# Squares of batch 2's first eight chunks taken by channel behind the first blocks, and the first group of x issued ahead of the third expert's weights

## The chip, the cores and the metric

The kernel runs on one core of a Trainium2 chip. The metric is the device time of one execution in microseconds (us), a median of several runs. The engines are TensorE (PE, with PEld for its weight loads), VectorE (DVE), ScalarE (ACT), GpSimd (POOL) and SyncE (SP), which here issues all ordinary DMAs in one queue, in program order. POOL issues the indirect DMAs (scatters).

## The reference, cut to what matters

```python
# q, k, v: (4, 5056, 256) f32; tau scalar; w_gate (256, 8); w1 (8, 256, 1024); w2 (8, 1024, 256)
qn = q / (np.linalg.norm(q, axis=1, keepdims=True) + 1e-06)   # by channel, over the 5056 tokens
kn = k / (np.linalg.norm(k, axis=1, keepdims=True) + 1e-06)
a = softmax(kn.transpose(0, 2, 1) @ qn / tau)                 # (4, 256, 256)
x = (v @ a).reshape(20224, 256)
expert_idx = np.argmax(x @ w_gate, axis=1)
for e in range(8):
    xe = x[expert_idx == e]
    out[expert_idx == e] = gate_w * (np.maximum(xe @ w1[e], 0.0) @ w2[e])
```

## The kernel before, in words

**Attention.** For each batch, `attention` loads q and k in 20 chunks of 256 tokens (`raw`, 512 KB each, L205). PE adds each chunk's products into two accumulators `sp` (L225 for a chunk taken as it is in f32, L229 and L230 for a chunk that is first split into a high and a low part `hl` by ACT, L188, and DVE, L189). For the norms ACT squares every chunk (L215 or L217) and DVE adds the squares into `ssq` (L218); after the last chunk PE sums `ssq` over the partitions (`ntp`, L245), so the norm is one number for each channel. A softmax follows, and then ten groups of 512 tokens of x: PE makes four tiles `px` (L365 for the first batch), ACT copies them and takes their squares (L370, L372), ACT and DVE write the two halves of the rows (L386, L387), some small DVE operations route the tokens (L395 to L442), and POOL scatters the rows to `xs` in HBM (L445).

**Weights.** `weights` loads eight experts in 32 loads of 512 KB (L120), 4 for an expert. PE takes a gram matrix of each (L158), DVE and PE make a scale from it (L162, L123, L84), and ACT and DVE split the weights in place in sixteen steps (L112 and L113).

**Blocks.** Tokens sorted by expert are run in blocks of 256: SP reads a table entry (L581), then loads the rows transposed (`xT`, L586) and their factors (`mt`, L588). A block has 48 `hp` products (L616), 48 `y` products (L638), ACT's and DVE's `ht` (L623, L624), ACT's `o` (L651) and two scatters to `out` by POOL (L653). `xT` and `mt` have three buffers each: the fourth block's `xT` waits for the first block's `hp`, its `mt` for the first block's scatters.

**Order.** The program is written as generators. In the opening each step takes one step of the first batch's attention (a group of x takes two steps, its half groups), then a number of weight loads, then, from step 23 on, a chunk of batch 2. The first block needs the first six groups of x, all weights and a table (`ctp`, L505). The remaining chunks of batch 2 are spread over the first three blocks. A scheduler then orders each engine's instructions. The `raw` and `vraw` tiles of batch 2 and of the first batch's last groups of x share one ring of three buffers (`RAW = 3`), taken strictly in turn; a load into a buffer waits on SP until its last reader is done, and all later loads of SP wait behind it. In the text chunks of batch 2 are numbered from 0; chunks 0 and 14 to 19 are split, chunks 1 to 13 are not.

The lines that set the opening's order and the chunk's work are these:

```python
second = attention(1, [i == 0 or i >= NATIVE for i in range(nch)], True, normal)
...
weighed += take(wts, 0 if step < nch else min(14 if step == nch else 2, 4 * E + 1 - weighed))
...
raw = work.tile([P, 2, 512], F32, tag=tag, name="raw", bufs=bufs)
load = sync.dma_start(out=raw, in_=qk[b, ch])
```

Of the kernel before, what the change touches and what calls it, by code (L numbers as in the profile page):

```python
# [10 lines left out]
F32 = mybir.dt.float32  # L11
F32R = mybir.dt.float32r
F16 = mybir.dt.float16
BF16 = mybir.dt.bfloat16
I32 = mybir.dt.int32
AF = mybir.ActivationFunctionType
ALU = mybir.AluOpType
AX = mybir.AxisListType
ENG = mybir.EngineType

P = 128
B, N, C = 4, 5056, 256
NP = 5120
E, F = 8, 1024
# [3 lines left out]
BLK = 256  # L28
G = 10
T = 4  # L30
CUT = 6

SORTED = [CUT * T * P] + [N * (b + 1) for b in range(B)]
# [27 lines left out]


@with_exitstack
def attention_then_experts(ctx, tc, qk, vT, wts_in, kc, out):
    nc = tc.nc
    sync, act, vec, pool, pe = nc.sync, nc.scalar, nc.vector, nc.gpsimd, nc.tensor

# [112 lines left out]
    RAW = 3  # L180
    WP = 5
    EARLY = 2
    NATIVE = 14
# [5 lines left out]
        vec.tensor_tensor(out=hl[:, 1], in0=raw, in1=hl[:, 0], op=ALU.subtract)  # L189
        return hl  # L190

    def attention(b, s_split, x_split, acc):

# [5 lines left out]
        for ch in range(nch):  # L201

            tag, bufs = (("raw", RAW), ("rows", 3), ("xg", 2), ("raw", RAW), ("rows", 3))[ch % 5 if b == 0 else 0]
            raw = work.tile([P, 2, 512], F32, tag=tag, name="raw", bufs=bufs)
            load = sync.dma_start(out=raw, in_=qk[b, ch])  # L205
            if b == 0:
                last_load[0] = load.ins
            hl = None
            if s_split[ch]:
                hl = split(raw)  # L210
                sq = raw
            else:
                sq = work.tile([P, 2, 512], F32, tag="hl", name="sq", bufs=2)
            if ch == 0:
                act.activation(ssq, raw, AF.Square)  # L215
            else:
                act.activation(sq, raw, AF.Square)  # L217
                vec.tensor_tensor(out=ssq, in0=ssq, in1=sq, op=ALU.add)  # L218
            def products(ch=ch, raw=raw, hl=hl):
                for j in range(2):  # L220
                    first, last = ch == 0 and j == 0, ch == nch - 1 and j == 1
                    for c in range(2):
                        kc0 = C + c * P
                        if not s_split[ch]:
                            pe.matmul(  # L225
                                sp[c][:, 0, :], raw[:, j, kc0 : kc0 + P], raw[:, j, 0:C], start=first, stop=last
                            )
                            continue
                        pe.matmul(sp[c], hl[:, 0, j, kc0 : kc0 + P], hl[:, :, j, 0:C], start=first, stop=False)  # L229
                        pe.matmul(  # L230
                            sp[c][:, 1, :], hl[:, 1, j, kc0 : kc0 + P], hl[:, 0, j, 0:C], start=False, stop=last
                        )


            if b > 0 or ch < nch - 2:
                products()
            else:
                behind.append(products)
            yield 2 * 640
# [10 lines left out]
            return tiny.tile([P, 4], F32, name=name)  # L250

        ss, y, h = four("n_ss"), four("n_y"), four("n_h")
        vec.tensor_scalar(out=ss, in0=tp[:, 0:4], scalar1=1e-30, scalar2=None, op0=ALU.max)

        vec.tensor_scalar(
            out=y.bitcast(I32), in0=ss.bitcast(I32), scalar1=-0.5, scalar2=float(0x5F3759DF), op0=ALU.mult, op1=ALU.add
# [408 lines left out]
    def take(gen, n):  # L665
        for _ in range(n):
            next(gen, None)
        return n
# [2 lines left out]
    normal = [(ps_a, "acc")] * 2  # L671
    wts = weights()
    first = attention(0, [False] * nch, False, [(ps_y, "y0"), (ps_y, "y1")])
    second = attention(1, [i == 0 or i >= NATIVE for i in range(nch)], True, normal)

    ones16 = one.tile([P, P], F16, name="ones16")
    vec.memset(ones16, 1.0)
# [28 lines left out]
    weighed = 0  # L706
    for step in range(2, nch + 1 + 2 * CUT):
        take(first, 1)
        weighed += take(wts, 0 if step < nch else min(14 if step == nch else 2, 4 * E + 1 - weighed))
        if step > nch + 2:  # L710
            take(second, 1)
    tables = {0: table(0)}
# [85 lines left out]
```

## Time and profile before

| | us |
|---|---|
| median of 3 runs | 1186.41 |
| lowest and highest | 1183.15, 1186.71 |
| the profiled execution | 1188.32 |
| its span, first to last instruction | 1186.6 |
| PE busy in the span | 1153.5 (97%) |
| PE busy from 240 to 1180 us | 936.50 of 940 |
| PE busy from 40 to 139.5 us | 82.01 of 99.5 |
| start of the first block on PE | 139.49 |
| start of batch 2's norm sum on PE (`ntp`) | 191.48 |

The table's busy times are read from the profile by stretch. A PE that is busy nearly all the time after 240 us means that work moved there is paid for in full, and that a delay before it is carried to the end.

### The profile page before, as it was taken

The page shows a single profiled execution, that of the slowest core. Times are in us where ns is not written, and L with a number is a line of the kernel's source. Part 1 is how long each engine was busy: PE and PEld are TensorE (multiplying, and loading weights), DVE is VectorE, ACT ScalarE, POOL GpSimd, SP SyncE. Part 2 cuts the span into 40 slices and gives each one's busy share as a digit, 9 for nine tenths or more (in the row PEclk, how much of TensorE's full clock was granted, in tenths as well). Part 3 has the DMA queues.
Part 4 walks back from the last instruction along what each step waited for, and adds up shares of the span by engine and source line. Part 5 has one row for each costly group of instructions (what it writes and reads, how often), then busy time and mean ns, then how long its engine had stood idle before and what let it go on. Part 6 is the DMA issues. An engine that isn't in the chain of part 4 may idle for free.

```text
span 1186.6 us, 28182 instructions
## 1 busy us (share of the span) xinstructions
PE 1153.5 (97%) x10242; PEld 1024.9 (86%) x10242; DVE 899.4 (76%) x2384; ACT 643.5 (54%) x1362; POOL 392.3 (33%) x366
## 2 busy tenths in 40 slices
PE   9798899999999999999999999999999999999998
PEld 8677688899888889999888889999988888889897
DVE  6789988778887877777888777776875566656886
ACT  6399854877655536665565536666533223332232
POOL 0046761466511123544422212455421111112121
PEclk9989989999999999999999999999999999999999
DMA  9977765445555524444354434443242222111121
GB/s 340 408 277 254 208 177 134 135 122 145 139 145 120 130 81 101 118 115 119 97 152 127 131 91 93 131 95 82 70 109 50 50 55 55 46 51 38 40 52 35
DMA packets 147871, 145.93 MB, mean 123 GB/s; under 512 B 115980, under 2 KB 117393, under 8 KB 147728
## 3 DMA queue, kind: packets, MB, share of 16 engines
q1 hardware_dynamic: 132336, 102.48, 33.0%
q0 software_dynamic: 15392, 41.60, 9.8%
q8 instruction: 82, 1.34, 0.5%
q14 instruction: 61, 0.50, 0.1%
HBM read 80.03 MB, written 43.29 MB: 104 GB/s over the span
## 4 chain that ended last, share of the span: by engine, by line
PE 57%; issue 24%; DVE 7%; POOL 5%; ACT 3%; DMA 3%; SPq 1%; POOLq 0%; DVEq 0%; ACTq 0%
PE y L638 20%; PE hp L616 19%; PE px L368 7%; POOL out L653 4%; PE sp L225 4%; PE sp L229 3%; DMA raw<-in_qk 2%; PE sp L230 2%; DVE W L113 1%; ACT xjunk L372 1%; PE px L365 1%; DVE rows L387 1%; DVE hl L189 1%; ACT W L112 1%; ACT xg L370 1%
## 5 line engine op out<-in xcount | busy, mean ns | idle before, releaser
L616 PE MATMUL hp<-xT,wp 128*128 128x256 f16 (+1 forms) x4320 | 450.0, 262 | 1.6 <-DVE ht L624 1.1
L638 PE MATMUL y<-wp,ht 128*128 128x256 f16 x3888 | 447.7, 273 | 0.0
L616 PEld LDWEIGHTS <-wp 128*128 128x128 f16 x4320 | 383.1, 98 | 46.1 <-issue 3.4
L638 PEld LDWEIGHTS <-ht 128*128 128x128 f16 x3888 | 373.9, 98 | 53.3 <-issue 4.7
L653 POOL DMA_INDIRECT out<-o,mt x162 | 184.9, 1141 | 628.5 <-ACT o L651 595.2
L604 DVE COPY wp<-W 128x1024 f16 x720 | 297.8, 425 | 116.0 <-PE y L638 65.3
L623 ACT ACTIVATE ht<-hp 128x512 f16<-128x512 f32 x324 | 191.6, 593 | 157.1 <-PE hp L616 143.1
L624 DVE SCALAR_TENSOR_TENSOR ht<-hp,ht 128x512 f16<-128x512 f32 x324 | 219.6, 686 | 22.6 <-ACT ht L623 16.6
L445 POOL DMA_INDIRECT xs<-rows,r_si x160 | 189.5, 1184 | 122.7 <-issue 41.8
L651 ACT ACTIVATE o<-y,b_fac 128x256 f32<-128x256 f32 x162 | 68.8, 470 | 207.2 <-PE y L638 196.6
L368 PE MATMUL px<-a_h,hl 128*128 128x264 f32 x480 | 98.1, 296 | 0.0
L386 ACT ACTIVATE rows<-xg,x_sc 128x256 f16<-128x256 f32 x160 | 69.9, 497 | 25.7 <-DVE r_ex L419 16.0
L368 PEld LDWEIGHTS px<-a_h,hl 128*128 128x128 f32 x480 | 78.8, 188 | 1.6 <-issue 0.6
L189 DVE TENSOR_TENSOR hl<-raw,hl 128x1024 fp32r<-128x1024 f32 x47 | 57.4, 1221 | 26.7 <-ACT hl L188 26.7
L188 ACT CAST hl<-raw 128x1024 fp32r<-128x1024 f32 x47 | 49.1, 1044 | 45.2 <-PE sp L230 38.2
L229 PE MATMUL sp<-hl 128*128 128x512 f32 x188 | 72.3, 418 | 1.1 <-DVE hl L189 1.1
L225 PE MATMUL sp<-raw 128*128 128x256 f32 x264 | 65.3, 403 | 7.5 <-DMA raw<-in_qk 7.5
L387 DVE SCALAR_TENSOR_TENSOR rows<-xg,x_sc,rows 128x256 f16<-128x256 f32 x160 | 69.5, 477 | 1.2 <-ACT rows L386 0.8
L217 ACT ACTIVATE raw<-raw 128x1024 f32<-128x1024 f32 x44 | 46.6, 1058 | 42.6 <-DVE hl L189 42.4
L372 ACT ACTIVATE xjunk<-xg 128x256 bf16<-128x256 f32 x160 | 66.7, 417 | 3.2
L368 PE MATMUL px<-a_l,hl 128*128 128x264 f32 x240 | 68.2, 284 | 0.0
L225 PEld LDWEIGHTS sp<-raw 128*128 128x128 f32 x264 | 52.0, 202 | 15.9 <-DMA raw<-in_qk 8.6
(144 smaller groups left out, 926.4 us busy)
## 6 DMA issues: line engine op xcount, KB each, us to landing
raw<-in_qk SPq DMA_DIRECT2D x80, 512.0 KB, 4.2
vraw<-in_vT SPq DMA_DIRECT2D x34, 512.0 KB, 5.1
W<-in_w SPq DMA_DIRECT2D x28, 512.0 KB, 8.5
v<-in_vT SPq DMA_DIRECT2D x12, 256.0 KB
out<-o,mt POOLq DMA_INDIRECT x162, 2.4
xs<-rows,r_si POOLq DMA_INDIRECT x160, 4.0
wraw<-in_w SPq DMA_DIRECT2D x4, 512.0 KB, 6.5
xT<-xs SPq DMA_TRANSPOSE x90, 3.9
```

The source lines that it names most:

```text
L225: pe.matmul(sp[c][:, 0, :], raw[:, j, kc0 : kc0 + P], raw[:, j, 0:C], start=first, stop=last)
L229: pe.matmul(sp[c], hl[:, 0, j, kc0 : kc0 + P], hl[:, :, j, 0:C], start=first, stop=False)
L368: pe.matmul(px, hl[:, vh, c, ts], ah[:, c, :], start=(n == 0), stop=(n == 5))
L372: act.activation(junk, xg[:, t, 0:C], AF.Square, accum_out=ss[:, t : t + 1])
L387: vec.scalar_tensor_tensor(out=r16[:, t, C : 2 * C], in0=x, scalar=sc[:, t : t + 1], in1=r16[:, t, 0:C], op0=ALU.mult, op1=ALU.subtract,)
L445: ins = pool.indirect_dma_start(out=xs[:, :], out_offset=bass.IndirectOffsetOnAxis(ap=si[:n, t : t + 1], axis=0), in_=rows[:n, t, :], in_o ...
L604: copied[0] = vec.tensor_copy(out=t, in_=Wf[:, ds(e * 8192 + n * 1024, 1024)]).ins
L616: pe.matmul(hp[:, f % nf, :], wp[:, dc, wh, (f % 2) * P : (f % 2 + 1) * P], xT[:, 2 * xh + dc, :], start=(n == 0), stop=(n == 5),)
L623: act.activation(ht[:, 0], hp, AF.Relu)
L624: vec.scalar_tensor_tensor(out=ht[:, 1], in0=hp, scalar=0.0, in1=ht[:, 0], op0=ALU.max, op1=ALU.subtract)
L638: pe.matmul(ys[j], hts[f // nf][:, hh, f % nf, j * P : (j + 1) * P], wp[:, f % 2, wh, :], start=(f == 0 and n == 0), stop=(f == 7 and n == 2),
L653: pool.indirect_dma_start(out=out[:, :], out_offset=bass.IndirectOffsetOnAxis(ap=mt.bitcast(I32)[:, j, 1:2], axis=0), in_=o, in_offset=Non ...
```

## The change

**Squares by channel.** Batch 2's chunks 0 to 7 no longer get a square on ACT and an add on DVE. Instead q and k of these eight chunks (2048 tokens) are stored a second time, transposed, as `qkT`: channels in partitions, 1024 tokens in a row. `own_squares` loads such a tile `row` (512 KB, in the same ring as `raw`), and ACT squares it in place and sums along the row (`accum_out`) into `parts`. It is called eight times, behind the load of chunks 10 to 17. After the chunks `parts` is reduced by one small DVE operation and added to the norm sum. Chunk 8 starts `ssq`, chunk 9 is the first to add.

**Chunk 0.** It is no longer split. The accumulators are cleared by a product of a zero tile `none` (one DVE memset, two f16 products of 512 columns) in place of the first product's start.

**Order of the opening.** Ten weight loads instead of fourteen stand ahead of the first group of x, then two loads twice, and three loads at each further step instead of two.

```diff
+ASIDE = 8
...
+    parts = tiny.tile([P, 4, 2], F32, name="n_parts", bufs=1)
+
+    def own_squares(n):
+
+        row = work.tile([P, ASIDE * P], F32, tag="raw", name="row", bufs=RAW)
+        sync.dma_start(out=row, in_=qkT[n // 2, n % 2])
+        act.activation(row, row, AF.Square, accum_out=parts[:, n // 2, n % 2 : n % 2 + 1])
+
+    def attention(b, s_split, x_split, acc, aside=0):
...
-            else:
+            elif ch >= aside:
                 sq = work.tile([P, 2, 512], F32, tag="hl", name="sq", bufs=2)
-            if ch == 0:
+            if ch == 0 and aside:
+                none = work.tile([P, 512], F16, tag="o", name="none", bufs=2)
+                vec.memset(none, 0.0)
+                for s_ in sp:
+                    pe.matmul(s_.rearrange("p s c -> p (s c)"), none[:, 0:P], none, start=True, stop=False)
+            if aside and nch - 10 <= ch < nch - 2:
+                own_squares(ch - (nch - 10))
+            if ch == aside:
                 act.activation(ssq, raw, AF.Square)
-            else:
+            elif ch > aside:
                 act.activation(sq, raw, AF.Square)
                 vec.tensor_tensor(out=ssq, in0=ssq, in1=sq, op=ALU.add)
...
-                    first, last = ch == 0 and j == 0, ch == nch - 1 and j == 1
+                    first, last = ch == 0 and j == 0 and not aside, ch == nch - 1 and j == 1
...
+        if aside:
+            vec.tensor_reduce(out=h, in_=parts, axis=AX.X, op=ALU.add)
+            vec.scalar_tensor_tensor(out=ss, in0=tp[:, 0:4], scalar=1e-30, in1=h, op0=ALU.max, op1=ALU.add)
...
-    second = attention(1, [i == 0 or i >= NATIVE for i in range(nch)], True, normal)
+    second = attention(1, [i >= NATIVE for i in range(nch)], True, normal, ASIDE)
...
-        weighed += take(wts, 0 if step < nch else min(14 if step == nch else 2, 4 * E + 1 - weighed))
+        weighed += take(wts, 0 if step < nch else min(10 if step == nch else 2 if step < nch + 3 else 3, 4 * E + 1 - weighed))
```

**Where the instructions stand.** On SP, at the start of the blocks, the last load of x of the first batch (`vraw`) was followed by chunk 10, and then came the first block's loads:

```order
L349 DMA vraw_1567<-in_vT 128x1024
L205 DMA raw_1708<-in_qk 128x1024
L581 TENSOR_LOAD c_tb_1333
L586 ISA
L586 DMA_TRANSPOSE xT_1339<-xs_78 128x4x256
```

Now the first block's loads come directly, and chunk 10 (`raw_1683`) is issued only after the third block's:

```order
L607 DMA_TRANSPOSE xT_1637<-xs_78 128x4x256
L609 ISA
L609 DMA mt_1639<-xs_78 128x2x2
L215 DMA raw_1683<-in_qk 128x1024
L198 DMA row_1686<-in_qkT 128x1024
L215 DMA raw_1731<-in_qk 128x1024
```

So chunk 10 has moved behind the loads of three blocks, while on PE its products stand behind the first 12 `hp` products both before and now.

On SP, between the third block's `mt` and the fourth block's `mt`, there stood before seven loads of chunks (11 to 17):

```order
L588 DMA mt_1664<-xs_78 128x2x2
L205 DMA raw_1753<-in_qk 128x1024
L205 DMA raw_1797<-in_qk 128x1024
L205 DMA raw_1835<-in_qk 128x1024
L205 DMA raw_1896<-in_qk 128x1024
L581 TENSOR_LOAD c_tb_1333
L586 ISA
L586 DMA_TRANSPOSE xT_1892<-xs_78 128x4x256
L205 DMA raw_1947<-in_qk 128x1024
L205 DMA raw_2011<-in_qk 128x1024
L205 DMA raw_2065<-in_qk 128x1024
L588 ISA
```

Now a `row` stands behind each chunk (the first five of the eleven loads of this stretch are shown with the fence above and this one):

```order
L198 DMA row_1734<-in_qkT 128x1024
L215 DMA raw_1778<-in_qk 128x1024
L602 TENSOR_LOAD c_tb_1308
L607 ISA
L607 DMA_TRANSPOSE xT_1879<-xs_78 128x4x256
L198 DMA row_1781<-in_qkT 128x1024
L215 DMA raw_1819<-in_qk 128x1024
L198 DMA row_1822<-in_qkT 128x1024
L215 DMA raw_1883<-in_qk 128x1024
L198 DMA row_1888<-in_qkT 128x1024
L215 DMA raw_1937<-in_qk 128x1024
L609 ISA
```

Chunks 16 and 17, which stood ahead of the fourth block's `mt`, have moved behind it.

On DVE, ahead of the first table (`c_ni`), the sixth group's routing ended so, with a step of the weights' split and an add of squares between the group's one-hot rows and its slots `r_si`:

```order
L416 TENSOR_REDUCE r_ex<-r_ex 128x8
L433 RECIPROCAL rows<-r_z 128x4
L113 SCALAR_TENSOR_TENSOR W<-W,scales 128x8x256
L218 TENSOR_TENSOR ssq<-ssq,sq 128x1024
L439 TENSOR_TENSOR r_sl<-rtp,r_ex 128x32
L442 TENSOR_REDUCE r_si<-r_sl 128x4
L507 SCALAR_TENSOR_TENSOR c_ni<-ctp,kt 1x8
```

Now it reads:

```order
L437 TENSOR_REDUCE r_ex<-r_ex 128x8
L452 TENSOR_REDUCE r_z<-r_d 128x4
L460 TENSOR_TENSOR r_sl<-rtp,r_ex 128x32
L453 SCALAR_TENSOR_TENSOR r_z<-r_z,x_sc 128x4
L463 TENSOR_REDUCE r_si<-r_sl 128x4
L454 RECIPROCAL rows<-r_z 128x4
L528 SCALAR_TENSOR_TENSOR c_ni<-ctp,kt 1x8
```

The last two splits of the weights now stand ahead of this group, and one add (chunk 9's) is left in it.

## Rows read from the trace of the kernel before

**Rows 1.** Busy time by stretch: PE, PEld, DVE, ACT, POOL, granted clock, DMA.

```profile
40.00:58.00 18.00, 9.46 (x120) 8.24 (x118) 14.45 (x41) 7.24 (x8) 0.00 (x0) 0.93 1.03 404
58.00:125.20 67.20, 58.94 (x386) 49.05 (x387) 60.90 (x151) 62.77 (x126) 40.07 (x24) 0.92 0.75 265
139.50:191.50 52.00, 48.06 (x357) 40.29 (x356) 43.28 (x115) 30.72 (x57) 28.00 (x22) 0.93 0.68 182
240.00:1180.00 940.00, 936.50 (x8700) 839.15 (x8699) 701.71 (x1850) 476.17 (x1023) 296.64 (x289) 1.00 0.36 94
```

**Rows 2.** Groups from 58 to 125.2 us: busy us, mean ns, idle before.

```profile
L113 DVE SCALAR_TENSOR_TENSOR W<-W,scales 128x2048 f16<-128x2048 f32 x11 | 25.7, 2348 | 1.1 <-ACT W L112 0.8 <-DMA W<-in_w 0.2
...
L218 DVE TENSOR_TENSOR ssq<-ssq,sq 128x1024 f32<-128x1024 f32 x8 | 9.8, 1220 | 0.0
L217 ACT ACTIVATE sq<-raw 128x1024 f32<-128x1024 f32 x9 | 9.5, 1055 | 0.2 <-DVE W L113 0.2
```

**Rows 3.** DVE in order of time, sixth group's routing: start, us, instruction.

```profile
114.87 0.18 DVE L395 TENSOR_REDUCE r_m<-xg 128x4 f32<-128x32 f32 x1
...
118.71 1.21 DVE L218 TENSOR_TENSOR ssq<-ssq,sq 128x1024 f32<-128x1024 f32 x1
...
120.57 2.32 DVE L113 SCALAR_TENSOR_TENSOR W<-W,scales 128x2048 f16<-128x2048 f32 x1
...
124.16 0.19 DVE L442 TENSOR_REDUCE r_si<-r_sl 128x4 int32<-128x32 f32 x1
...
125.93 2.35 DVE L113 SCALAR_TENSOR_TENSOR W<-wraw,scales,W 128x2048 f16<-128x2048 f32 x1
```

**Rows 4.** POOL in order of time: the sixth group's scatters.

```profile
125.22 0.96 POOL L445 DMA_INDIRECT xs<-rows,r_si  x1 [0.36 <-ACT W L112]
126.48 2.63 POOL L445 DMA_INDIRECT xs<-rows,r_si  x1 [0.30 <-ACT xg L370]
...
130.68 0.96 POOL L445 DMA_INDIRECT xs<-rows,r_si  x1 [0.30 <-issue]
```

**Rows 5.** The chain of waits around the first block: start, us, what.

```profile
115.58 4.37 DMA raw<-in_qk
...
130.68 5.07 DMA xs<-rows,r_si
135.90 1.34 SPq L586
...
143.04 5.36 DMA raw<-in_qk
```

**Rows 6.** PE in order of time, at the first block and batch 2's norm sum.

```profile
139.49 1.47 PE L616 MATMUL hp<-xT,wp 128*128 128x256 f16 x12
140.80 1.89 PE L225 MATMUL sp<-raw 128*128 128x256 f32 x8
...
142.78 2.78 PE L616 MATMUL hp<-xT,wp 128*128 128x256 f16 x24
148.44 3.78 PE L225 MATMUL sp<-raw 128*128 128x256 f32 x8 [2.88 <-DMA raw<-in_qk]
...
191.48 0.95 PE L245 MATMUL ntp<-ones,ssq 128*128 128x1 f32 x8
```

**Rows 7.** SP's queue in order of time: loads of the ring.

```profile
157.97 0.34 SPq L205 DMA_DIRECT2D raw<-in_qk  x1
...
165.58 0.33 SPq L205 DMA_DIRECT2D raw<-in_qk  x1
...
174.49 0.39 SPq L588 DMA_DIRECT2D mt<-xs  x1
```

**Rows 8.** What SP's queue waited for, 125 to 192 us: us, times, longest.

```profile
SPq L205 <- PE sp L225: 12.3, 3, 6.6
SPq L588 <- DMA out<-o,mt: 12.3, 2, 8.4
```

**Rows 9.** The tile raw, 60 to 200 us: ns min/median/max, and landing.

```profile
L188 ACT CAST hl<-raw x7: 1033/1045/1054, 75.8 to 183.2; 128x1024 fp32r<-128x1024 f32 x7
L189 DVE TENSOR_TENSOR hl<-raw,hl x7: 1203/1212/1226, 77.0 to 184.2; 128x1024 fp32r<-128x1024 f32 x7
L217 ACT ACTIVATE raw<-raw x6: 1052/1058/1062, 162.9 to 185.5; 128x1024 f32<-128x1024 f32 x6
L218 DVE TENSOR_TENSOR ssq<-ssq,raw x6: 1205/1211/1226, 164.3 to 186.8; 128x1024 f32<-128x1024 f32 x6
...
DMA to landing us min/median/max: 3.7/4.5/8.9
```

More of the change, by code (lines that the diff above doesn't have):

```diff
@@ L63, in attention_then_experts @@
 @with_exitstack
-def attention_then_experts(ctx, tc, qk, vT, wts_in, kc, out):
+def attention_then_experts(ctx, tc, qk, qkT, vT, wts_in, kc, out):
     nc = tc.nc
@@ L190, in split @@
         return hl
-    def attention(b, s_split, x_split, acc):
+    parts = tiny.tile([P, 4, 2], F32, name="n_parts", bufs=1)
[4 more added lines that the diff above has]
+    def attention(b, s_split, x_split, acc, aside=0):
         sp = [pool_.tile([P, 2, C], F32, tag=tag, name=f"sp{c}") for c, (pool_, tag) in enumerate(acc)]
@@ L252, in attention @@
         ss, y, h = four("n_ss"), four("n_y"), four("n_h")
-        vec.tensor_scalar(out=ss, in0=tp[:, 0:4], scalar1=1e-30, scalar2=None, op0=ALU.max)
+        if aside:
+            vec.tensor_reduce(out=h, in_=parts, axis=AX.X, op=ALU.add)
+            vec.scalar_tensor_tensor(out=ss, in0=tp[:, 0:4], scalar=1e-30, in1=h, op0=ALU.max, op1=ALU.add)
+        else:
+            vec.tensor_scalar(out=ss, in0=tp[:, 0:4], scalar1=1e-30, scalar2=None, op0=ALU.max)
         vec.tensor_scalar(
@@ L781 @@
     w2 = np.asarray(moe_w2).reshape(E, 8, P, C).transpose(0, 2, 1, 3).reshape(E, P, 2, 1024)
+    qk = np.ascontiguousarray(qk.transpose(0, 2, 1, 3, 4, 5)).reshape(B, NP // P // 2, P, 2, 2 * C)
     arrays = {
-        "qk": np.ascontiguousarray(qk.transpose(0, 2, 1, 3, 4, 5)).reshape(B, NP // P // 2, P, 2, 2 * C),
+        "qk": qk,
+        "qkT": np.ascontiguousarray(qk[1, :ASIDE].reshape(2, ASIDE * P, 4, P).transpose(2, 0, 3, 1)),
         "vT": np.ascontiguousarray(vT.transpose(0, 1, 4, 3, 2)),
```

## The prediction

> **What bounds the kernel now.** I read the busy times by stretch first [rows 1]. From 240 us on PE is busy for 936.5 of 940 us: whatever moves the point at which this steady part begins moves the end by as much. Before it PE has holes. From 40 to 58 us it is busy for 9.46 of 18 us, from 58 to 125.2 us for 58.94 of 67.2 us at a granted clock of 0.92, and in the first blocks, 139.5 to 191.5 us, for 48.06 of 52 us at 0.93. In the same 67.2 us DVE is busy for 60.90 and ACT for 62.77: these two set the pace of the opening, 91% and 93% busy, and not PE. The chain of waits [rows 5] then says what the first block waits for: the sixth group's scatter has landed at 135.75 us, SP issues the first `xT` at 135.90, and the blocks follow. It ends in a load of a chunk, issued at 143.04 and landed at 148.40, for which PE stands idle for 2.88 us [rows 6]. So two things must be costed: how much sooner the first `xT` is issued, and what the ring of three buffers does from there to the norm sum at 191.48 us [rows 6], behind which the order of PE is the same as before.
>
> **The opening, a gain of 6.** The eight squares and their adds leave a stretch in which ACT and DVE are the bound. An add takes 1.22 us, a square 1.06 us, a step of the weights' split 2.35 us on DVE [rows 2]. I follow the sixth group. On DVE its routing begins at 114.87 and its slots are ready at 124.16 us, 9.5 us with the last operation's own time; in between stand three adds (one at 118.71) and a split at 120.57 [rows 3]. The new order keeps one add there and no split: 9.5 - 2 x 1.22 - 2.32 = 4.7 us, so 4.7 us are gained if the routing begins when it did. Its four scatters took from 125.22 to 131.64, and the second of them lasted 2.63 us, against 0.96 for its neighbour, just while a split ran on DVE from 125.93 [rows 3, 4]; with the splits done earlier I take 1.7 us off. Together 6.4 us.
>
> Does the routing begin when it did? On DVE five adds and the split of chunk 0 leave the time ahead of it (6.1 + 1.2 us), two steps of the weights' split come into it (4.7 us): 2.6 us sooner. On ACT seven squares and one cast leave (8.4 us), two split steps of about 2.0 us and chunk 8's square come in (5.0 us): 3.4 us sooner. Against it stands that three engines are now equally loaded and wait for each other more; DVE was idle for 6.3 of the 67.2 us, ACT for 4.4 [rows 1], and twice that would eat this whole gain. I count the start as unchanged less a little waiting and take **-6.0 us** for the issue of the first `xT`, with -2 and -10 as bounds (all waiting doubled; 6.4 with the 3.4 us of ACT). The first group of x in front of the third expert belongs to the same sum: it fills the hole of PE between 40 and 58 us, but PE is not what the opening waits for, so it is worth only what it takes off ACT's and DVE's idle time, and it is in the bounds. The idle 4.37 us of [rows 5] at 115.58 is likewise inside the 9.5 us and not counted again.
>
> **Chunk 10 behind three blocks' loads, a loss of 4.6.** SP issues three blocks' loads from 135.90 to 142.9 us and the next chunk at 143.04 [rows 5], 7.1 us after the first `xT`. Before, PE had 12 `hp`, chunk 10 and 24 more `hp` to do until that chunk (11) landed, and still waited for 2.88 us [rows 6]. Now the chunk so loaded is number 10, and in front of it PE has 12 `hp` only. The load lands as late as before, so the 24 `hp` and a chunk, 2.78 + 1.89 = 4.7 us less the overlap of two records, are done after it and not ahead of it: **+4.6 us** against the issue of the first `xT`. PE runs cold behind the hole before and after: chunk 11 took 3.78 us where chunk 10 took 1.89 [rows 6], so that part cancels. Bounds: 0, if x's products now end later than the first `xT` lands and fill the hole, and 6, if the longer idle time keeps PE at the lower clock for longer.
>
> **The ring, a loss of 7.** A chunk's buffer is in use for the landing, 4.5 us in the median, and its readers [rows 9]. A chunk that is not split needs PE's 1.89 us: 6.4 us. A split one needs cast, subtraction, square and add, 1.05 + 1.21 + 1.06 + 1.21: 9.0 us. A `row` needs its landing and one square: 5.6 us. Before, nine chunks (11 to 19) passed from 143.04 to 191.48, 48.4 us: 3 x 6.4 + 6 x 9.0 = 73 us in three buffers, 24 us, half of the time. Now 4 x 6.4 + 6 x 9.0 + 8 x 5.6 = 124 us, 41.5 us in each buffer. That fits in 48.4 only if nothing stops the queue. SP's queue does stop: for 12.3 us on PE's products and for 12.3 us, 8.4 at the longest, on the `mt` of blocks whose buffers the scatters to `out` still hold [rows 8]; the fourth block's `mt` was issued at 174.49 although the load ahead of it went at 165.6 [rows 7]. Before, chunks 15 to 17 had been issued ahead of that `mt` (the first at 157.97, [rows 7]), and now chunks 16 and 17, with two `row`s, stand behind it. With these stops, 41.5 + 12.3 = 53.8 us, 5.4 too many. Going through SP's and ACT's new order by hand, buffer by buffer with landings of 4.0 to 4.5 us, I get more: chunk 14 late by 1.5 us, 16 by 2.4, 17 by 2.9, then 18 and 19, some 11 to 12 us in sum. A `row` also stands in ACT's queue ahead of other blocks' `ht`, so a late `row` holds PE twice. With the shortest landing of 3.7 us it is 110 us in three buffers, 36.7, and with the stops 49: a loss of 1. I take **+7 us**, between 5.4 and 11.5 and nearer the former, since the nearest row for the stops is the measured one; bounds 1 and 12.
>
> [...]
>
> **The rest, nothing.** The two zero products and the unsplit chunk 0 add under 1 us to PE in the opening, where DVE and ACT are the bound; without that cover it would be +0.7. The small reduction of `parts` (one operation on 128x8 numbers, like the routing's of 0.2 us) stands on DVE in batch 2's norm chain, while PE has blocks to do. The 4 MB more from HBM fall into a stretch whose DMA engines are busy for 0.68 [rows 1]. Memory traffic is thus no bound in itself; the turn of three buffers is.
>
> **Sum.** -6.0 + 4.6 + 7.0 = +5.6 us. The profiled execution took 1188.3 us, 1.9 more than the median; 1188.3 + 5.6 - 1.9 = **1192.0 us**. Its own range, from the bounds of the ring and half of those of the opening, is 1189 to 1200. Within 0.3% means 1182.9 to 1190.0, about what a measurement of this kernel can tell from no change.
>
> **Rivals.** (1) The ring keeps up. It was full but idle half of the time, and the eighth and ninth groups' routing no longer stands as far back among the blocks' products, so POOL may free the `mt` sooner. Then the ring costs 1, chunk 10 costs 3, and the opening yields 9: -5, 1181.4 us, faster. It decides where, besides short landings, SP's stop at the fourth block's `mt` is under 4 us. For it speaks how busy ACT and DVE were; against it that the new order leaves no load ahead of PE. (2) Gain and loss cancel: the loads land in about 3.7 us as the shortest do [rows 9], the ring costs 1 and the rest is as forecast: -6.0 + 4.6 + 1 = -0.4, 1186.0; it decides where the landings stay under 4 us, and against it stands the median of 4.5. [...] (3) The ring loses by the hand count, 11.5, and the opening yields 2 to 4: +13, 1199; ACT's order, with `row` ahead of `ht`, is its mechanism. That the squares would not leave the opening is excluded: the listing has one add left ahead of the first table.
>
> **How the numbers follow.** The forecast, slower by 3.6 to 10 us, gets 0.42; (3) 0.10; (2), with everything inside 0.3%, 0.24; (1), with everything that is faster, 0.24. Slower is thus 0.52. The range leaves out the far end of (1) and of (3), together under 0.2: 1181 to 1200.
>
> **What would show it.** The opening: the first `xT` on SP at about 130 us, the sixth group's slots 5 us or so sooner, no scatter of that group over 2 us. Chunk 10: PE idle for 5 to 7 us behind the first 12 `hp`, with the load `raw` as the releaser. The ring: PE waits of 1 to 4 us in front of chunks 14 to 19, released by the cast or subtraction of a chunk that was loaded late; SP waiting on `row`'s square and on scatters. The norm sum of batch 2 at about 197 us in place of 191.5. I would be wrong if the first `xT` came before 126 us, or if PE stood for less than 3 us in the first three blocks.

## The result, and the profile after

The changed kernel takes 1199.59 us in the median of 4 runs (1199.15 to 1200.03), the kernel before 1186.56 us in the same comparison: a ratio of 1.010, with a 95% interval from 1.0077 to 1.0122, 13.0 us more. The profiled execution took 1200.03 us, its span is 1198.3 us.

Busy time by stretch, changed kernel (columns as in [rows 1]):

```profile
40.00:58.00 18.00, 14.47 (x118) 12.22 (x116) 13.95 (x37) 10.13 (x18) 0.00 (x0) 0.81 1.03 403
58.00:125.20 67.20, 58.83 (x408) 48.75 (x406) 56.07 (x164) 55.82 (x119) 35.24 (x25) 0.95 0.76 268
139.50:191.50 52.00, 41.24 (x277) 32.94 (x278) 30.04 (x86) 28.61 (x48) 17.48 (x16) 0.87 0.73 221
240.00:1180.00 940.00, 935.53 (x8640) 837.72 (x8639) 700.52 (x1857) 480.15 (x1041) 300.68 (x293) 1.00 0.37 95
```

Against [rows 1], DVE and ACT are relieved in the opening (56 us of 67.2 each, where they had 61 and 63), and the steady part is the same. The time went in the first blocks: PE is busy for 41.2 of 52 us there, 6.8 us less than before, at a lower granted clock.

DVE in order of time, around the sixth group's routing (answers to [rows 3]):

```profile
110.47 2.35 DVE L114 SCALAR_TENSOR_TENSOR W<-W,scales 128x2048 f16<-128x2048 f32 x1
...
116.74 2.35 DVE L114 SCALAR_TENSOR_TENSOR W<-wraw,scales,W 128x2048 f16<-128x2048 f32 x1 [3.76 <-ACT W L113]
119.01 0.18 DVE L416 TENSOR_REDUCE r_m<-xg 128x4 f32<-128x32 f32 x1
119.10 1.21 DVE L235 TENSOR_TENSOR ssq<-ssq,sq 128x1024 f32<-128x1024 f32 x1
...
123.21 0.19 DVE L463 TENSOR_REDUCE r_si<-r_sl 128x4 int32<-128x32 f32 x1
```

The routing itself is as short as forecast, 4.2 us from the first operation to the last in place of 9.3, but it begins 4.1 us later than in [rows 3]. DVE stood for 3.76 us ahead of the last split, for ACT's half of it. On ACT that half stands behind a copy of `px`, and the copy waited for PE:

```profile
114.43 0.38 ACT L391 COPY xg<-px 128x264 f32<-128x264 f32 x1 [1.89 <-PE px L386]
114.70 2.00 ACT L113 ACTIVATE W<-wraw,scales 128x2048 f16<-128x2048 f32 x1
```

PE's queue had two chunks ahead of that product. The slots are ready 0.95 us sooner, and the four scatters take 0.96 to 1.24 us each (2.63 at the longest in [rows 4]). SP's queue in order of time (answers to [rows 5] and [rows 7]):

```profile
132.65 1.35 SPq L607 DMA_TRANSPOSE xT<-xs  x1
...
139.82 0.41 SPq L215 DMA_DIRECT2D raw<-in_qk  x1
140.32 0.42 SPq L198 DMA_DIRECT2D row<-in_qkT  x1
140.83 0.38 SPq L215 DMA_DIRECT2D raw<-in_qk  x1
150.22 0.33 SPq L198 DMA_DIRECT2D row<-in_qkT  x1
152.76 0.33 SPq L215 DMA_DIRECT2D raw<-in_qk  x1
```

The first `xT` goes 3.25 us sooner than in [rows 5]. Then three loads fill the ring, and SP's queue stands for 9 us. PE in order of time (answers to [rows 6]), with batch 2's first product of x as the last row:

```profile
145.02 2.93 PE L242 MATMUL sp<-raw 128*128 128x256 f32 x6 [7.11 <-DMA raw<-in_qk]
...
163.98 3.11 PE L242 MATMUL sp<-raw 128*128 128x256 f32 x8 [2.09 <-DMA raw<-in_qk]
...
183.19 0.50 PE L246 MATMUL sp<-hl 128*128 128x512 f32 x1 [1.76 <-DVE hl L190]
...
188.90 0.50 PE L246 MATMUL sp<-hl 128*128 128x512 f32 x1 [1.09 <-DVE hl L190]
...
201.66 1.05 PE L262 MATMUL ntp<-ones,ssq 128*128 128x1 f32 x8
...
218.26 0.37 PE L389 MATMUL px<-a_h,hl 128*128 128x264 f32 x1
```

SP's stand of 9 us goes back to chunk 10. PE stood for 7.11 us until that chunk had landed, and a routing's small products (`rtp`) are queued on PE behind it. DVE was idle for 8.98 us until these were done and ACT for 8.72 us until DVE was, and the square of the first `row` is queued on ACT behind that (PE, then ACT):

```profile
147.74 0.23 PE L444 MATMUL rtp<-r_ex,tri 128*128 128x32 f16 x1
```

```profile
148.93 0.23 ACT L431 ACTIVATE r_d<-r_d 128x32 f32<-128x32 f32 x1 [8.72 <-DVE r_eq L421]
149.06 1.04 ACT L199 ACTIVATE row<-row 128x1024 f32<-128x1024 f32 x1
```

The load of the second `row` goes at 150.22, when this square is done. It thus takes the first `row`'s buffer and not that of chunk 10, which ACT squares only from 151.69 us: the ring is not taken quite as strictly in turn as the description of the kernel says.

What SP's queue waited for from 125 to 202 us (us, times, longest; answers to [rows 8]), then what ACT sat idle for ahead of the squares of `row` (us, times), and the landing of the tile `raw` (answers to [rows 9]):

```profile
SPq L198 <- ACT row L199: 14.4, 3, 8.9
SPq L609 <- DMA out<-o,mt: 10.1, 2, 6.0
SPq L215 <- ACT row L199: 5.3, 2, 3.2
```

```profile
  DMA row<-in_qkT: 10.4, 6
```

```profile
DMA to landing us min/median/max: 3.6/4.6/4.8
```

So SP's loads stood for 19.7 us behind squares of `row`, 8.9 of them in that one stand, and ACT for 10.4 us behind landings of `row`. From the first `xT` to the norm sum PE does the same work as before (372 products, 373 before). It is not busy for 14.4 us of this stretch, 4.6 before, and busy for 54.6 us, 51.0 before, at a granted clock of 0.90 in place of 0.94. The 11.7 us between the two profiled runs divide thus: the first `xT` -3.25; from it to the norm sum 69.0 us in place of 55.6, +13.4; from the norm sum to the first product of x 16.6 in place of 15.4, +1.2; from there to the end 980.0 in place of 979.8.

### The profile page after: what moved, and what is told of

Its sections match the earlier page's. It is cut to its first block, busy times and chain, and to the rows that moved or that the text cites. A ratio compares the mean times of both kernels' runs of the same rounds, so it can differ in the third digit from the quotient of the medians.

```text
span 1198.3 us, 28188 instructions
## 1 busy us (share of the span) xinstructions
PE 1159.3 (97%) x10244; PEld 1026.2 (86%) x10244; DVE 889.6 (74%) x2377; ACT 643.6 (54%) x1369; POOL 379.9 (32%) x366
## 4 chain that ended last, share of the span: by engine, by line
PE 54%; issue 24%; DVE 9%; POOL 4%; ACT 4%; DMA 3%; SPq 1%; POOLq 0%; DVEq 0%; ACTq 0%
PE y L659 18%; PE hp L637 18%; PE px L389 6%; POOL out L674 4%; PE sp L242 4%; PE sp L246 3%; DVE W L114 2%; DMA raw<-in_qk 2%; PE sp L247 2%; ACT W L113 1%; DMA row<-in_qkT 1%; DVE rows L408 1%; DVE ht L645 1%; DVE wp L625 1%; ACT xjunk L393 1%
## 5 line engine op out<-in xcount | busy, mean ns | idle before, releaser
L674 POOL DMA_INDIRECT out<-o,mt x162 | 182.5, 1127 | 648.1 <-ACT o L672 615.0
L466 POOL DMA_INDIRECT xs<-rows,r_si x160 | 182.9, 1143 | 131.1 <-issue 41.9
L242 PE MATMUL sp<-raw 128*128 128x256 f32 x272 | 66.5, 402 | 9.2 <-DMA raw<-in_qk 9.2
L242 PEld LDWEIGHTS sp<-raw 128*128 128x128 f32 x272 | 53.4, 200 | 17.8 <-DMA raw<-in_qk 10.3
```

What stands on the lines that cost most here:

```text
L242: pe.matmul(sp[c][:, 0, :], raw[:, j, kc0 : kc0 + P], raw[:, j, 0:C], start=first, stop=last)
L466: ins = pool.indirect_dma_start(out=xs[:, :], out_offset=bass.IndirectOffsetOnAxis(ap=si[:n, t : t + 1], axis=0), in_=rows[:n, t, :], in_o ...
L674: pool.indirect_dma_start(out=out[:, :], out_offset=bass.IndirectOffsetOnAxis(ap=mt.bitcast(I32)[:, j, 1:2], axis=0), in_=o, in_offset=Non ...
```

## The experiments

Two kernels' places are compared below rather than their ends alone. In the comparison of e1 to e4 the kernel before itself took 1215.2 us, in that of e5 to e8 1224.9 us; these are called the two long comparisons below. Most of the additional time lies behind 240 us, where nothing was changed: in the traces of e1 to e8 PE is busy for 914 to 919 of 940 us there, in all others for 934 or more. This is e2's row:

```profile
240.00:1180.00 940.00, 919.38 (x8345) 817.60 (x8343) 682.70 (x1808) 471.55 (x1015) 296.41 (x286) 1.00 0.35 94
```

A part of it lies ahead of that. Where a kernel has a trace of both kinds, the first product of x comes later in the long comparison, by 2.0 us (e2 against e18), 2.9 us (e1 against e17) and 4.1 us (e5 against the changed kernel). And the first `xT` of e9 and e15, which have the opening of the kernel before, is 2.9 us apart. So differences of under 3 us between two traces decide nothing alone, and e1 to e8 are best compared with each other.

The table gives, from each trace, the issue of the first `xT`, the norm sum's distance behind it, batch 2's first product of x, and the ratio to the kernel before of the same comparison.

| run | what | first `xT` | norm sum behind it | first product of x | ratio (95%) |
|---|---|---|---|---|---|
| before | | 135.9 | 55.6 | 206.8 | |
| e12 | before again | 137.3 | 54.8 | 207.5 | 0.9996 (0.9984 to 1.0009) |
| after | | 132.7 | 69.0 | 218.3 | 1.010 (1.0077 to 1.0122) |
| e5 | after again | 131.2 | 74.6 | 222.4 | 1.0090 (1.0064 to 1.0117) |
| e1 | order alone | 136.7 | 59.1 | 211.7 | 1.0069 (1.0037 to 1.0100) |
| e17 | order alone | 139.3 | 53.6 | 208.8 | 1.0020 (1.0000 to 1.0040) |
| e2 | squares alone | 129.2 | 66.5 | 212.2 | 1.0021 (1.0000 to 1.0042) |
| e18 | squares alone | 128.2 | 65.5 | 210.2 | 1.0055 (1.0037 to 1.0073) |
| e3 | after without rows | 132.4 | 57.7 | 205.4 | 0.9970 (0.9951 to 0.9989) |
| e8 | squares alone, no rows | 129.8 | 57.2 | 202.6 | 0.9904 (0.9874 to 0.9934) |
| e9 | before, rows in the ring | 137.6 | 65.7 | 219.7 | 1.0124 (1.0104 to 1.0143) |
| e15 | before, rows in x's buffers | 134.7 | 60.5 | 210.9 | 1.0091 (1.0061 to 1.0121) |
| e4 | after, rows in x's buffers | 132.4 | 62.2 | 210.0 | 1.0051 (1.0029 to 1.0073) |
| e6 | squares alone, x's buffers | 129.9 | 61.7 | 207.9 | 0.9977 (0.9953 to 1.0001) |
| e13 | e6, loads without squares | 128.2 | 59.4 | 203.3 | 1.0004 (0.9985 to 1.0023) |
| e14 | e6, squares without loads | 128.9 | 63.3 | 208.0 | 1.0173 (1.0146 to 1.0199) |
| e10 | after, short squares | 131.6 | 65.3 | 212.6 | 1.0077 (1.0058 to 1.0096) |
| e7 | after, chunk 10 first | 134.7 | 62.0 | 211.8 | 1.0014 (0.9992 to 1.0035) |
| e11 | e6, loads by ACT's queue | 129.2 | 61.2 | 206.4 | 1.0015 (1.0001 to 1.0028) |
| e16 | e6, five buffers, late | 129.6 | 63.3 | 208.6 | 1.0035 (1.0017 to 1.0053) |

The two kernels themselves once more (no edit), e12 and e5:

> The kernel before itself once more, for a trace beside those of this chip: no difference, within 0.3%; first xT at 136 us and norm sum 55 to 56 us behind it, if the slower chip's loss lies behind 240 us, and later ones if it lies ahead.

> The changed kernel itself once more, beside the next three and against the same runs of the kernel before: 11 to 14 us slower than the kernel before, first xT at about 132.6 us, norm sum 69 us behind it.

Both times held (e5 was 12.2 us slower); e5's norm sum came later than given, with 5.0 us of PE's waiting at chunk 13.

### The two parts apart

The order of the loads alone, twice:

```diff
-        weighed += take(wts, 0 if step < nch else min(14 if step == nch else 2, 4 * E + 1 - weighed))
+        weighed += take(wts, 0 if step < nch else min(10 if step == nch else 2 if step < nch + 3 else 3, 4 * E + 1 - weighed))
```

> The kernel before with the new order of the weights' loads alone (ten loads, then two twice, then three a step); the squares stay where they were, no row is loaded. Theory A (the loss is made between the first xT and the norm sum of batch 2, by chunk 10's late load and by the eight row tiles in the ring of three): ACT and DVE carry the same work in the opening, chunk 10 is still loaded ahead of the first xT, so the time stays at 1186.5 within 2 us. Rival B (the order of the loads is what costs, since the sixth group's routing begins 4.2 us later with it): 1190 or more, with the first xT issued after 138 us. If the order by itself is what gained 3.3 us at the first xT: about 1183, first xT at about 132.6.

> The kernel of e1 once more: the kernel before with the new order of the weights' loads alone. If the order by itself costs what e1 said: 5 to 9 us slower than the kernel before, batch 2's first x product at 211 to 213 us (206.8 before). If that was the call's: within 2 us of the kernel before.

e1 came out 0.7% slower, e17 0.2%, 2.7 us by the medians. The traces agree that nothing is gained: the first `xT` is no sooner than in the kernel before. I take e17's size, since nothing slowed the stretch behind 240 us there. In e17 chunk 10 is still loaded ahead of the first `xT` (at 133.19 us, the `xT` at 139.27).

The squares alone is the changed kernel with the line above turned back, also twice:

> The changed kernel with the old order of the weights' loads (fourteen, then two a step). Chunk 10's load then stands ahead of the first xT again, as in the kernel before; the eight rows stay. Theory A: the stall at chunk 10 (7.1 us of PE idle in the changed kernel) goes, worth 4 to 5 us; the ring's loss of about 9 us stays: 1192 to 1195, norm sum about 64 us behind the first xT. Rival C (PE's wait at chunk 10 is covered by other waits, the rows alone set the end): 1198 to 1200. Rival B (order of loads): at or under 1188.

> The kernel of e2 once more: the changed kernel with the old order of the weights' loads. From the pieces measured since (rows in the ring 12.2 us at batch 2's first x product by e9, the opening and its lost squares -4.6 by e8): 7 to 8 us slower than the kernel before. By e2 itself: 2 to 4 us slower.

e18 was 6.5 us slower (e2: 4.1), its first product of x 3.4 us later than before. DVE, then SP's queue, in e18:

```profile
109.88 0.17 DVE L416 TENSOR_REDUCE r_m<-xg 128x4 f32<-128x32 f32 x1
...
114.19 0.19 DVE L463 TENSOR_REDUCE r_si<-r_sl 128x4 int32<-128x32 f32 x1
...
121.64 2.35 DVE L114 SCALAR_TENSOR_TENSOR W<-wraw,scales,W 128x2048 f16<-128x2048 f32 x1 [1.93 <-ACT W L113]
...
127.14 0.18 DVE L592 TENSOR_SCALAR c_tb<-c_sf 1x5 int32<-1x5 f32 x1
```

```profile
128.23 1.33 SPq L607 DMA_TRANSPOSE xT<-xs  x1
```

With the old order the sixth group's slots are ready 10 us sooner than in [rows 3], since the last two splits stand behind them and not ahead. The first `xT` gains 7.7 of these: the last split now lies within the first table's arithmetic, which ends at 127.1. The new order gives 4.4 us of it back (132.65 against 128.23). The order costs 2.0 us at the first product of x when it is alone (e17) and 8.0 on top of the squares (after against e18): 4.4 at the first `xT`, and 3.6 behind it, where chunk 10's load has fallen behind the blocks' loads, which the order alone does not do. The long comparisons give 4.9 (e1 against the kernel before) and 10.2 (e5 against e2) at that product. Their ends do not show it: 0.7% for the order alone, and 0.9% less 0.2% on top of the squares.

### What the rows cost

The kernel before with the eight rows added and nothing taken out (e9, the first hunk), and the same with their tiles outside the ring (e15, the second hunk on top of it):

```diff
+            if b == 1 and nch - 10 <= ch < nch - 2:
+                own_squares(ch - (nch - 10))
...
-        row = work.tile([P, ASIDE * P], F32, tag="raw", name="row", bufs=RAW)
+        row = work.tile([P, ASIDE * P], F32, tag="xg", name="row", bufs=2)
```

> The kernel before, nothing moved or taken out, with the eight row loads added in the ring of three and their squares on ACT (the sums are not used). This prices the rows by themselves. Theory R (the price is the turn of the ring and of SP's queue: 17 loads behind the first xT in place of 9): first xT as before, norm sum 64 to 67 us behind it in place of 55.6, 8 to 11 us slower. Rival H (the rows cost only because the changed kernel reaches its blocks sooner and PE is then ahead of SP anyway): under 4 us slower.

> The kernel before with the eight rows added as in e9, but in the two buffers of x's groups and not in the ring. If the ring is the larger part of the 13.8 us of e9, as 69.0 against 62.2 us (the changed kernel against e4) says: 4 to 7 us slower than the kernel before, norm sum 59 to 60 us behind the first xT. If the ring is not what counts: 11 to 14 us slower.

PE in order of time in e9, then in e15:

```profile
203.23 0.95 PE L255 MATMUL ntp<-ones,ssq 128*128 128x1 f32 x8
...
219.67 0.37 PE L378 MATMUL px<-a_h,hl 128*128 128x264 f32 x1
```

```profile
195.19 0.95 PE L255 MATMUL ntp<-ones,ssq 128*128 128x1 f32 x8
...
210.91 0.49 PE L378 MATMUL px<-a_h,hl 128*128 128x264 f32 x2
```

The rows by themselves cost 13.8 us, 12.2 at the first product of x (against e12), as much as the whole change. Outside the ring they cost 7.4 us by the medians (10.8 by the ratio), 3.4 to 4.1 at that product. So the ring's part is 5.2 us in the norm sum's distance and 8.8 at the first product of x, and rival H, by which the rows cost only behind an earlier `xT`, falls.

The changed kernel without rows (e3), and the same with the old order of loads (e8):

```diff
-            if aside and nch - 10 <= ch < nch - 2:
-                own_squares(ch - (nch - 10))
+    vec.memset(parts, 1.0)
```

> The changed kernel without the eight row loads and their squares (the norm of batch 2 then lacks its first eight chunks). Theory A: the first xT stays at about 132.6 us; the ring's loss goes (about 9 us), the stall at chunk 10 stays: 1188 to 1191, norm sum 59 to 61 us behind the first xT (55.6 before, 69.0 with the change). Rival D (the cold PE and the stall at chunk 10 are the whole loss, rows cost little): 1196 or more.

> The changed kernel with the old order of the loads and without the eight row loads and their squares (the norm of batch 2 lacks its first eight chunks): what taking the squares out of the opening is worth by itself. Theory A2: first xT at about 129 us, norm sum 55 to 57 us behind it, 5 to 8 us faster than the kernel before. Rival G (a gain at the first xT is lost behind it, since PE has work of x's groups left to do): under 3 us faster.

PE in e3, in order of time:

```profile
144.53 1.96 PE L241 MATMUL sp<-raw 128*128 128x256 f32 x6 [4.38 <-DMA raw<-in_qk]
...
190.08 0.95 PE L261 MATMUL ntp<-ones,ssq 128*128 128x1 f32 x8
```

It waits at chunk 10 as the changed kernel does, if for less time, and still has its norm sum 57.7 us behind the first `xT`, 11.3 us less than the changed kernel and only 0.5 more than e8, which has no such order. e8 shows what the opening is worth when nothing follows it: 4.3 us at the first product of x. By the medians it is 10.6, but of a long comparison, so the place counts. Of the 6.2 us by which its first `xT` is sooner 1.9 are lost again by then, which is a part of what rival G said.

Rows in x's two buffers, on the changed kernel (e4) and with the old order (e6); the edit is the tag of e15:

> The changed kernel with the row tiles in the two buffers that x's groups use at other times, and not in the ring of three; same loads, same squares on ACT. Theory A (the turn of three buffers): nearly as without rows, 1189 to 1193, PE waits in front of chunks 12 to 19 under 1 us each. Rival E (ACT's order: a row's square ahead of a block's ht holds PE, whatever buffer it is in; rival 3 of the prediction): 1196 to 1199, PE waiting on hp and y for ht.

> The changed kernel with the old order of the weights' loads and with the row tiles in the two buffers of x's groups. Theory A2 (three separate causes: the order of the loads takes back 3.5 us of a gain of 6.8 at the first xT, it costs about 2 more at chunk 10, and the ring of three costs about 7; a rest of some 4.5 us is the squares' own place on ACT): first xT at about 129 us, norm sum 58 to 61 us behind it, 2 to 5 us faster than the kernel before. Rival F (the rows cost 11 us wherever their tiles lie, and it is the DMA traffic or ACT): 2 to 5 us slower, norm sum 65 us or more behind the first xT.

e4 has its norm sum 6.8 us nearer than the changed kernel (whose own two traces are 5.6 apart), e6 3.7 nearer than e18. Both keep a loss of 4.5 us against the same kernel without rows (62.2 against 57.7, 61.7 against 57.2). That is neither theory whole: in the changed kernel the ring is the larger part of the rows' price (6.8 of 11.3 us), with the old order the smaller (3.7 of 8.3).

### The rest: traffic or ACT

e6 with the loads but no squares (e13), and with the squares but no loads (e14):

```diff
-        act.activation(row, row, AF.Square, accum_out=parts[:, n // 2, n % 2 : n % 2 + 1])
```

```diff
-        sync.dma_start(out=row, in_=qkT[n // 2, n % 2])
+        pool.memset(row, 1.0)
```

> The kernel of e6 (old order of the weights' loads, rows in the two buffers of x's groups) with the eight row loads but without their squares (left out of batch 2's norm). Theory T (traffic or SP's queue makes the rest of the rows' price): as e6, 0 to 3 us faster than the kernel before. Theory S (the squares on ACT, ahead of casts and ht, make it): as without rows, 8 to 11 us faster, norm sum 57 us behind the first xT.

> The kernel of e6 with the eight squares on ACT but without the loads: POOL fills each row with ones in its place (so batch 2's norm counts ones for its first eight chunks). Theory S (the squares on ACT): as e6, 0 to 3 us faster than the kernel before. Theory T (traffic, or waiting for a row's landing): 7 to 10 us faster, norm sum 57 to 58 us behind the first xT.

PE in e13, in order of time:

```profile
187.62 0.95 PE L262 MATMUL ntp<-ones,ssq 128*128 128x1 f32 x8
...
203.27 0.37 PE L389 MATMUL px<-a_h,hl 128*128 128x264 f32 x1
```

Its first product of x is 4.7 us sooner than e6's and 0.7 later than e8's, its norm sum's distance (59.4) midway between theirs (61.7 and 57.2). e6 and e8 are of a long comparison, and in e8's trace PE has a wait of 3.4 us at chunk 11 that the profile gives no reason for. Against e14, e11 and e16 below, which have the squares and are not of a long comparison, e13's first product of x is 3.1 to 5.3 us sooner. So the squares on ACT cost some 2 to 5 us; the 4 MB and their place in SP's queue cost 0.7 to 2.2 by these rows, and more if e8 was held up. By the medians e13 was only 1.2 us faster than the kernel before, where 8 to 11 were given for the squares as the whole rest; its runs spread from 1183.0 to 1190.7 us, so that this end decides nothing.

e14's end can't be compared: with ones in the norm the tokens fall otherwise, and the run works through three blocks of half size more. The group of POOL's stores to `out` (count, busy us and mean ns, idle before) says so, first in e14, then in e13:

```profile
L674 POOL DMA_INDIRECT out<-o,mt x165 | 186.3, 1129 | 646.3 <-ACT o L672 613.1 <-issue 17.7 <-DVE wp L625 8.2
```

```profile
L674 POOL DMA_INDIRECT out<-o,mt x162 | 183.9, 1135 | 638.1 <-ACT o L672 605.1 <-issue 17.5 <-ACTq L778 4.3
```

Its first product of x, ahead of that, is where e6's is. How it gets there is the clearest picture of the mechanism; ACT, DVE and PE of e14 in order of time:

```profile
145.05 1.06 ACT L199 ACTIVATE row<-row 128x1024 f32<-128x1024 f32 x1 [6.45 <-POOL row L198]
```

```profile
146.69 1.67 DVE L408 SCALAR_TENSOR_TENSOR rows<-xg,x_sc,rows 128x256 f16<-128x256 f32 x4 [6.81 <-ACT rows L407]
```

```profile
148.75 0.17 PE L526 MATMUL ctp<-r_ex,ones 128*128 128x8 f16 x1 [4.49 <-DVE r_sl L460]
```

POOL fills the row late, behind its scatters. ACT stands 6.45 us in front of that square, with the tenth group's scaling queued behind it, DVE waits for the scaling, and PE for DVE. A late row stops all of them, here one that is filled late, in the changed kernel those that land late (ACT's 10.4 us). For the same reason e14 does not price the squares' bare time.

Short squares in the changed kernel (e10):

```diff
-        act.activation(row, row, AF.Square, accum_out=parts[:, n // 2, n % 2 : n % 2 + 1])
+        act.activation(row[:, 0:P], row[:, 0:P], AF.Square, accum_out=parts[:, n // 2, n % 2 : n % 2 + 1])
```

> The changed kernel with all its loads, but each row's square takes 128 of its 1024 columns (seven eighths of these squares are left out of batch 2's norm): ACT has some 7 us less to do, the order and the waits for landings stay. Theory R: a row holds its buffer for 0.9 us less of 5.6, in three buffers 8 x 0.9 / 3 = 2.4 us: 9 to 11 us slower than the kernel before. Rival ACT (the squares' time ahead of the blocks' ht and the chunks' casts holds PE; rival 3 of the prediction): the whole 7 us come back, 4 to 6 us slower.

It was 7.9 us slower than the kernel before by the medians, 9.1 by the ratio, and its first product of x is 5.7 us sooner than the changed kernel's. That lies between the two: more than the ring's 2.4 us, less than the whole of ACT's 7. Bare time and standing in line were not separated further.

### Chunk 10, and two attempts at a better kernel

One more chunk in the opening of the changed kernel (e7):

```diff
+    take(second, 1)
     tables = {0: table(0)}
...
-    START = -(2 * CUT - 2) * 2 * 640
+    START = -(2 * CUT - 1) * 2 * 640
```

> The changed kernel with one more chunk taken in the opening, so that chunk 10 (and the first row) is loaded ahead of the first blocks' xT. If the stall at chunk 10 is worth the 4.6 us of the prediction: 7 to 9 us slower than the kernel before, norm sum 64 us behind the first xT. Theory A2 (worth about 2 us, since the run without rows had the stall and lost only 2.1 against the kernel before): 10 to 12 us slower, norm sum 66 to 67 us behind the first xT.

1.9 us slower than the kernel before, 10.3 us better than e5 beside it, with a first `xT` 3.6 us later and a norm sum 12.6 us nearer to it. Both sizes given were far too small. The edit takes two loads, chunk 10 and the first row, out of the ring's queue behind the blocks: 16 remain of 18. And no square of a row now stands behind chunk 10's landing: SP stood for 9.9 us behind squares of `row`, in e5 for 18.6. Without rows a stall of 4.38 us at chunk 10 cost 0.5 us (e3 against e8). A late chunk is thus cheap alone and dear with rows in the ring, since it holds up the first row's square and with it SP's queue. As e7 moves a row along with the chunk, it does not price chunk 10 by itself.

The best of the pieces is e6, old order and x's buffers. Two ways to take the rest off it were tried: rows loaded from ACT's own queue and squared a chunk later (e11), and rows in five buffers, squared two or three chunks behind their load (e16).

```diff
-        sync.dma_start(out=row, in_=qkT[n // 2, n % 2])
+            act.dma_start(out=row_of[n], in_=qkT[n // 2, n % 2])
```

```diff
+    LOADS = {13: (0, 1), 14: (2,), 15: (3, 4), 16: (5,), 17: (6, 7)}
+    SQUARES = {15: (0,), 16: (1, 2), 17: (3,), 18: (4, 5), 19: (6, 7)}
...
+        tag, bufs = (("xg", 2), ("xg", 2), ("rows", 3), ("rows", 3), ("rows", 3))[n % 5]
```

> The kernel of e6 (old order of the weights' loads, row tiles in the two buffers of x's groups), with the rows loaded from ACT's queue, the next one behind the square that frees its buffer, so that SP's queue never stands behind a row. Theory R (what is left of the rows' price in e6, 4.5 us, is SP's queue standing on x's buffers ahead of the chunks): first xT at 129 to 130 us, norm sum 57 to 59 us behind it, 6 to 10 us faster than the kernel before. Rival (DMA traffic, or the squares' place on ACT): as e6, 1 to 3 us faster, norm sum 61 to 62 us behind the first xT.

> The kernel of e6 with the rows in five buffers that x's groups leave free (two of xg, three of rows), loaded beside chunks 13 to 17 and squared two chunks after the load, so that ACT finds each row landed. If ACT's waits for landings and SP's waits for the two buffers are the rest: 5 to 9 us faster than the kernel before, norm sum 58 us behind the first xT. If it is the squares' own time on ACT or the traffic: as e6, 0 to 3 us faster.

Neither helped. In e11 SP no longer stands behind a row, and the norm sum is as far behind as in e6. In e16 ACT waits for a row for only 0.7 us, but five rows and a `mt` stand ahead of chunks 16 and 17 on SP, and PE waits for chunk 16 (PE in order of time):

```profile
173.82 0.80 PE L256 MATMUL sp<-hl 128*128 128x512 f32 x1 [6.58 <-DVE hl L190]
```

No version beat the kernel before by more than the measurement can tell; with the squares left out altogether the ceiling is e8's.

## Why the prediction was right in sign and wrong in size

**The forecast** was +5.6 us on the profiled run, and it was +11.7; between the medians 13.0, since the profiled run of before lies 1.8 us over the median of its runs in this comparison and that of the changed kernel only 0.4. The mechanism was the one forecast: an earlier first `xT`, a stall at chunk 10, a ring that loses more than the opening gains. Of the 6.1 us that are missing 2.75 are the opening's and 2.9 the ring's, 1.5 came up behind the norm sum, and chunk 10 gave 1.0 back. The end is that of rival 3 (1199: the ring by the hand count, the opening at 2 to 4), and its terms are nearer than the forecast's: the ring 9.9 where it said 11.5, the opening 3.25.

**The opening**, -6.0, gave -3.25. The routing's length (4.7 us, measured 4.4 with the last operation's own time) and the scatters came as said. The first step that failed is "Does the routing begin when it did?", answered with unchanged. I had set busy time that leaves against busy time that comes in, engine by engine. But the two splits go from ACT to DVE through a queue that also holds copies of `px`, and PE was at chunks: the routing began 4.1 us later. e18 shows that the squares alone would have begun it 5.0 us sooner (109.88) and given -7.7. So the order of loads, which I had put into the bounds as worth nothing, took 4.4 us back, and it is also what moved chunk 10.

**Chunk 10**, +4.6: the stall is there, 7.11 us released by `raw`, just over the 5 to 7 named, and 4.2 more than the 2.88 at chunk 11 [rows 6] that went in exchange. Without rows it is worth 0.5 to 2.1 us (e3 against e8 and before): in e3 PE came to its first `hp` later (138.69) and stood for 4.38 us, 1.5 more than those 2.88. With the rows it is worth 3.6 (after against e18), and there it does something that the prediction did not have: through PE, DVE and ACT it makes the first `row`'s square late and shuts the ring for 8.9 us. The term was nearly right in size, in part for another reason. That PE's low clock cancels did not hold for the whole stretch: the same products took 3.6 us more from the first `xT` to the norm sum, and chunk 13, behind a hole of 2.09 us, took 3.11 us where chunk 10 took 1.89 in [rows 6]. How much of the 3.6 us is the clock's was not separated.

**The ring**, +7, gave 9.9 (e18: 65.5 against 55.6). This is the second step that failed, a mis-sized term. I had 5.4 by an average over three buffers and 11.5 by walking the queue buffer by buffer, and chose nearer the average because its stops were measured. The stops of the kernel before were the wrong row: SP stood for 12.3 us on `mt` there and for 10.1 after, but squares of `row` came on top, 13.4 us in e18 and 19.7 in the changed kernel, a wait that no trace of before could show. It is a circle: SP waits for ACT's square, and ACT (10.4 us) for the load. Of the 9.9 us the ring's buffers are 3.7 (e18 against e6), 4.5 come with the rows wherever they lie (e6 against e8), and 1.6 are there without rows (e8's 57.2 against 55.6). A part of the middle one is the squares' place on ACT, 2.3 by e13 against e6. The prediction had that as rival 3, "ACT's order, with `row` ahead of `ht`", at a chance of 0.10. PE's waits at chunks 14 to 19 are smaller than named, 4.0 us together and 1.76 at the most.

**The rest, nothing**: 1.2 us came up between the norm sum and the first product of x. PE waits there for DVE for 1.6 us, before for 0.55, which is 1.0 of it. e9 and e18 have it too (16.4 and 16.5 us against 15.4), e3, e4 and e7 don't (15.0 to 15.4); why DVE comes later was not found.

**The landings** of chunks were no relief: 3.6 us at the least and 4.6 in the median (3.7 and 4.5 in [rows 9]), so the condition of rival 2 (landings under 4 us) was not met. The 4 MB and their place in SP's queue, as traffic put at nothing, cost 0.7 us at the first product of x and 2.2 in the norm sum's distance (e13 against e8); traffic alone was not separated.

## What to carry over

A load that joins a ring on an in-order queue is priced by walking that queue, load by load with the buffer that each waits for; an average of buffer time hides that one late buffer stops everything behind it. Work that leaves a full stretch is not free in an emptier one if it must stand in line there ahead of what the bound engine waits for: ACT was busy for 31 of 52 us, and eight squares of 1.06 us still cost 2 to 5. A stall is followed through every engine that waits for the one that stands: chunk 10's ended, three engines on, in the queue of loads. A change of two parts is costed with each part alone and both together, since the order of loads cost 2 us alone and 8 on top of the squares.

## What the runs showed of the hardware

One thing was not expected: the kernel before, unchanged, took 1186.6 to 1187.5 us in four comparisons and 1215 and 1225 us in two others. It does not go with the chip: chip 15 gave 1215 in one comparison and 1187.5 in another, chip 13 gave 1225 and 1187.0. In e2's trace most of the additional time lies in the steady part, at a granted clock of 1.00 (PE busy for 919 us, 936 in the kernel before). The traces of e1 to e8 have waits that the profile puts down to "remote", and none of the other twelve has one. Why was not found. A place in the trace ahead of that part told the kernels apart better than their ends, if only to some 3 us.
